# The last 768 tokens' first four chunks as one job of 384-token blocks, in place of a 192-token tile and two 288-token jobs

## Chip, core and metric

The kernel runs on one core of a Trainium2 chip. The metric is the time of one execution on the device in microseconds (us); lower is better. Engines: PE (TensorE) multiplies, DVE (VectorE), ACT (ScalarE) and POOL (GpSimd) work element by element, SP issues the DMA transfers.

## What is computed

Three layers in a row, in float32: causal attention with a bias (4 batches, 8 heads, 576 tokens, 64 wide), then a gated layer with an RMS norm over 2304 tokens (512 to 1536 and back), then a second layer (512 to 2048 and back).

```
scores = q @ k.T / 8 + min(-(cum_i - cum_j), 0), causal; attn = softmax(scores) @ v
x   = attn as 2304 x 512;  xn = x / rms(x) * rms_g
y   = (silu(xn @ w_gate) * (xn @ w_val)) @ w_out
out = gelu_sigmoid(y @ w_in) @ w_out2
```

## The kernel before

Float32 operands are split into a rounded part and a remainder, so that a product is three PE instructions (`mm3`, `mul`). The first layer's 1536 inner columns are 12 chunks of 128; `G0` = 4 of them are done early, as *fill*: while the attention runs, PE takes `fa_tile` products of finished tokens between the heads' own. A fill tile (an entry of `TIN`) has 4 chunks, each with 8 gate and value steps and 4 output steps of three instructions, 144 in all. Tiles 0 to 5 have 256 tokens, the seventh has 192 (tokens 1536 to 1727, the rest of batch 2). A tile's result goes to `y_d` in DRAM through the copy `YO`.

The other tokens are done behind the attention. `TA` = 1728 tokens are covered by tiles; the last 576 are two jobs "R" of `RN` = 288 (`run_r`): gate and value products over 4 row blocks, an activation (`gate`, `gated`, `split_h`), and output products (`Down`), whose result passes through a ring of three buffers `RE` to `r_d`. Chunk 4 of tokens 0 to 767 is a plain job "P" with 384-token blocks, whose gate and value products stand partly among the last fill products. Two short products then clear banks 6 and 7 for what follows.

From there on the jobs of `SJ` run: a job is a layer, a part `p` of 768 tokens and some chunks. Each chunk takes seven block products (`Group`, m1 to m7) in place of eight, on pieces B11 to T4 of the tokens. `piece` makes a piece from `xT` at a part's first use and writes it to `pc_d`; later jobs load it. `load_y` reads a part's early result back into `xT`, to which the outputs are added. Weights come as 64-bit floats and are decoded by ACT, DVE and POOL (`decode`) into 17 slots; a unit is taken up when a slot is free (`tick`, `declare_w`).

The order of each engine's work comes from a planner (`plan`) that places all recorded operations by latest start times; `HD`, `FD` and `WD` are due times for heads, fill tiles and weights. What it chose is fixed in the built program. Profile lines all name L214, the one line through which operations are issued, so the tiles tell them apart: `w` and `s` after the comma are weights, `sc` and `sd` hold the fill's inputs, `sb`, `sf`, `sg`, `sh` the attention's.

```
"TIN": [(t * 256, 256) for t in range(6)] + [(1536, 192)],
RN = (NT - TA) // 2
jobs = [("P", 0, [G0]), ("R", 0, list(range(G0))), ("R", 1, list(range(G0)))] + SJ
```

Of the kernel before, what the change touches and what calls it, by code (L numbers as in the profile page):

```python
# [24 lines left out]
PRM = {  # L25
    "G0": 4, "NWS": 17, "NWO": 12, 
    "QF": set(range(10)), "VF": set(range(10)),
    "TIN": [(t * 256, 256) for t in range(6)] + [(1536, 192)],
    "PPB": 3, "PTB": 8, "XHB": 7, "HHB": 5,
    "VIRT": 260096,  # L30
    "SLOTS": {
# [14 lines left out]
    "TA": 229.33, "PASS": 0, "ISSUE": 0.45, "IDLE": 7, "PEN": {},  # L46
}


# [1 line left out]
def attention_then_swiglu_then_gelu(ctx: ExitStack, tc, qT, kT, vp, s, w1, w2, gT, out):  # L51
# [13 lines left out]
    NW, NWS = 3 * G0, PRM["NWS"]  # L65
    H2 = 384
    NP = NT // (2 * H2)
    RN = (NT - TA) // 2
    NAMES = ["B11", "T1", "T2", "B22", "T3", "B21", "T4"]


# [8 lines left out]
    pq = ctx.enter_context(tc.tile_pool(name="pq", bufs=1, space=PSUM))  # L80
    slots = ctx.enter_context(tc.tile_pool(name="slots", bufs=1, reuse_waits="tile"))
    PB = [pq.tile([P, 512], F32, tag=f"b{i}", name=f"b{i}") for i in range(8)]
    y_d = dram.tile([P, KT, TA], F32, tag="y_d", name="y_d")
    c_d = dram.tile([HB, S], F32, tag="c_d", name="c_d")
    ch_d = dram.tile([HB, 2, S], F32, tag="ch_d", name="ch_d")
    pc_d = {
        (l, p, nm): dram.tile([P, 4 * H2], F32, tag=f"pc{l}{p}{nm}", name=f"pc{l}{p}{nm}")
        for l in "12" for p in range(NP) for nm in NAMES
    }
    r_d = [dram.tile([P, KT, RN], F32, tag=f"r{i}", name=f"r{i}") for i in range(2)]  # L90

    def own(name, shape, dt=F32):
        return const.tile([P] + shape, dt, tag=name, name=name)
# [8 lines left out]
    def few(n):  # L102
# [8 lines left out]
    SHAPE = {  # L111
        "Q": [S], "K": [S], "mask": [S], "SQ": [S], "VS": [5, 2 * D], "PA": [1600], "PT": [512], "VP": [2, 5, 2, D],
        "BT": [320], "XH": [2, TS], "TH": [TS], "FH": [2, TS], "YO": [2, TS], "w": [2, 512], "wb": [512], "ws": [512],
        "MK": [2, 2, H2], "HH": [2, H2], "M5": [H2], "SG": [H2], "V1": [H2], "RE": [RN], **{nm: [2, 2, H2] for nm in NAMES},
    }
    ROUND = ("QA", "QB", "KA", "KB", "VP", "XH", "FH", "w", "HH", *NAMES)

# [49 lines left out]
    def get(name, n=None):  # L167
        if n is None:
            return BUF[name][0]
        return [BUF[f"{name}{i}"][0] for i in range(n)]  # L170
# [9 lines left out]
    PC = {nm: BUF[nm][0] for nm in NAMES}  # L180
    MK, HH, M5, SG = get("MK", 2), get("HH", 8), get("M5", 2), get("SG", 2)
    wb, ws, V1 = (get(x) for x in ("wb", "ws", "V1"))
    RE = get("RE", 3)
    FB = [PB[i] for i in PRM["FB"]]
    BB = [PB[i] for i in PRM["BB"]]

# [193 lines left out]
    def cp(o_, i_, scale=1.0, **kw):  # L380
        op("A", lambda e: e.activation(out=o_, in_=i_, func=AF.Copy, scale=scale), **kw)
# [10 lines left out]
    def dma(o_, i_, eng="S", **kw):  # L392
        op(eng, lambda e: e.dma_start(out=o_, in_=i_), dma=True, **kw)
# [528 lines left out]

    def load_y(p):
        lo, hi = p * 2 * H2, (p + 1) * 2 * H2
        n = min(hi, TA)
        dma(xT[:, :, lo:n], y_d[:, :, lo:n])
        if hi > n:
            for i in range(2):
                t0 = TA + i * RN
                dma(xT[:, :, t0:t0 + RN], r_d[i][:, :, :])  # L930

# [4 lines left out]
    def bank_():  # L936
        return bank_free.pop(0)

    def done(b):
        bank_free.append(b)  # L940

    def tmul(fn):
        op("T", fn, chain=True)
# [13 lines left out]

    hh = {}
    hh_i = [0]
    sg_i = [0]  # L960

    def split_h(key, src, n, psum):
        s = (0, 1, 2, 3, 0, 1)[hh_i[0]] if hh_i[0] < 6 else (hh_i[0] - 2) % 8
# [90 lines left out]
    class Down:  # L1054
# [30 lines left out]
        def finish(self, first, final):  # L1085
            self.part(self.chunks)
            b, p, o = self.b, self.p, self.o
            ps = FB[b]
            if self.layer == "R":
                q = o[1]  # L1090
                t = RE[(q + p * KT) % 3]
                cp(t[:, :RN], ps[:, :RN])
                dma(r_d[p][:, q, :], t[:, :RN])
            elif self.layer == "P":
                t, q = o
                mt = MK[t].rearrange("p a k n -> p (a k) n").bitcast(F32)
                add(mt[:, q, :], ps[:, :H2], mt[:, q, :])
                if q == KT - 1:
                    dma(y_d[:, :, (2 * p + t) * H2:(2 * p + t + 1) * H2], mt)
            elif self.layer == "1":  # L1100
                t, q = o
                y = xT[:, q, (2 * p + t) * H2:(2 * p + t + 1) * H2]
                add(y, ps[:, :H2], y)
            else:
                b0 = p * 2 * H2
                if o < 4:
                    v, src = xT[:, o, b0:b0 + 512], ps[:, :]
                else:
# [16 lines left out]
    for g in range(4):  # L1125
        for p in ((2, 1, 0) if g % 2 == 0 else (0, 1, 2)):
            SJ.append(("2", p, [2 * g, 2 * g + 1]))
    jobs = [("P", 0, [G0]), ("R", 0, list(range(G0))), ("R", 1, list(range(G0)))] + SJ

    def olist(layer, cs):  # L1130
        return [2 * x + y for x in cs for y in (0, 1)] if layer == "2" else cs
# [15 lines left out]

    step[0] = 1
    declare_w()
    for t in range(2):  # L1150
        mt = MK[t].rearrange("p a k n -> p (a k) n").bitcast(F32)
        dma(mt, y_d[:, :, t * H2:(t + 1) * H2])
    first = {"B11": "B11", "B21": "B21", "B12": "T1", "B22": "B22"}
    for nm in ("B11", "B21", "B12", "B22"):
        k, t = BL[nm]
        part2(PC[first[nm]], xv(k, 0, t))
    w = fw["1", G0, "f"]
    for t in range(2):
        bs = [bank_(), bank_()]
        for k, y in enumerate("12"):  # L1160
            for b, r in zip(bs, "12"):
                mul(FB[b], w["A" + r + y], first[f"B{y}{t + 1}"], k == 0, k == 1)
        i = gate(FB[bs[0]], H2)
        done(bs[0])
        gated((G0, t), i, FB[bs[1]], H2)
        done(bs[1])

    RX = [("T2", "T3"), ("T4", "B21")]

    def split_r(i):  # L1170
        t0 = TA + i * RN
        for k in range(2):
            part2(PC[RX[i][k]][:, :, :, :RN], xT[:, 2 * k:2 * k + 2, t0:t0 + RN])

    split_r(0)
    split_r(1)

    def ones():
        for i in range(2):
            tmul(lambda e, i=i: e.matmul(BB[i][:, :], WS[2][:, 0, 0:P], WS[2][:, 0, :], start=True, stop=True))  # L1180

    ones()
    tick()
    for o in [(t, q) for t in range(2) for q in range(KT)]:
        Down("P", 0, o, [G0], H2).finish(True, False)
# [7 lines left out]
        gi[0] += 1  # L1193
        return g

    def run_r(i, ahead):
        downs = [Down("R", i, (0, q), list(range(G0)), RN) for q in range(KT)]
        for c in range(G0):
            bs = []
            for u in range(2):  # L1200
                b = bank_()

                def fn(e, b=b, u=u, c=c):
                    for k in range(KT):
                        x = PC[RX[i][k // 2]]
                        mm3(e, FB[b][:, :RN], WS[3 * c + u], k * P, lambda a: x[:, a, k % 2, :RN], k == 0, k == KT - 1)

                tmul(fn)
                bs.append(b)
            g = gate(FB[bs[0]], RN)  # L1210
            done(bs[0])
            gated((c, 0), g, FB[bs[1]], RN)
            done(bs[1])
            tick()
            if (i, c) == (0, 0):
                for nm in ("B11", "T1", "B22"):
                    piece("1", SJ[0][1], nm)
            if (i, c) == (1, 0):
                for nm in ("T2", "T3"):
                    piece("1", SJ[0][1], nm)  # L1220
            if (i, c) == (1, G0 - 1):
                for nm in ("B21", "T4"):
                    piece("1", SJ[0][1], nm)
        for d in downs[:3]:
            d.part(list(range(G0 - 1)))
        for x, d in enumerate(downs):
            d.finish(True, False)
            for f in ahead.get(x, ()):
                f()
        tick()  # L1230

    run_r(0, {})
    nxt = new_group(SJ[0], 0)
    run_r(1, {0: (nxt.m1,), 1: (nxt.m5,), 2: (nxt.m6,)})
    seen = set()
    for j, job in enumerate(SJ):
        layer, p, cs = job
# [230 lines left out]
```

## Time and profile before

| what | value |
|---|---|
| timed runs, median of 3 | 1048.69 us (1047.87 to 1049.31) |
| the profiled execution: time, span | 1048.84 us, 1047.1 us |
| busy: PE, DVE, ACT, POOL | 1027.7, 704.5, 571.3, 409.9 us |
| instructions | 17466 |

The page's busy share is an average over stages with different limits. The kernel has an attention stage with fill (to about 359 us), a short join, the two "R" jobs (to about 409 us) and the jobs of seven products to the end; they are to be read stage by stage. A matmul's own duration in the trace covers its way through the array and overlaps the next; what one costs in a row of them is the distance between starts.

### The profile page before, as it was taken

To read this page: it belongs to the slowest core of one execution; us is meant where nothing else is said; L and a number is where in the kernel's file an instruction comes from. 1 tells how busy PE (TensorE), PEld (TensorE's weight loads), DVE (VectorE), ACT (ScalarE), POOL (GpSimd) and SP (SyncE) were. 2 spreads that over 40 slices of the span, in tenths; PEclk is the share of its full clock that TensorE was granted. 3 is DMA by queue.
4 is the path that set the end of the run, shared out by engine and by line. 5 is a ranking of instruction groups with operands and counts; after the bars stand their busy time and mean duration, and the time that the engine had idled before them with its cause. 6 is when DMAs were issued, how large, how long until landed. Compare 5 with 4: busy or idle time off the path is not lost.

```text
span 1047.1 us, 17466 instructions
## 1 busy us (share of the span) xinstructions
PE 1027.7 (98%) x6214; PEld 964.5 (92%) x6214; DVE 704.5 (67%) x1590; ACT 571.3 (55%) x1306; POOL 409.9 (39%) x482
## 2 busy tenths in 40 slices
PE   9997999999999999999999999999999999999998
PEld 5886999999999999999999999989999988999987
DVE  6776887778867757888754787876564376373333
ACT  5785886776667435565432444667663244453322
POOL 5656687665546513544310443632230042030000
PEclk9998999999999999999999999999999999999999
DMA  5457665564431645675454287766165237514551
GB/s 152 115 148 180 171 152 159 157 168 114 102 100 39 209 164 203 219 285 181 149 196 179 61 291 271 272 231 251 54 245 200 85 101 271 211 41 145 203 195 61
DMA packets 64639, 176.22 MB, mean 168 GB/s; under 512 B 7284, under 2 KB 26228, under 8 KB 64552
## 3 DMA queue, kind: packets, MB, share of 16 engines
q1 hardware_dynamic: 64440, 175.02, 50.6%
q8 instruction: 49, 0.80, 0.3%
q14 instruction: 38, 0.31, 0.1%
q10 hardware_dynamic: 112, 0.08, 0.0%
HBM read 111.34 MB, written 44.26 MB: 149 GB/s over the span
## 4 chain that ended last, share of the span: by engine, by line
PE 89%; DVE 3%; DMA 3%; POOL 1%; issue 1%; SPq 1%; ACT 0%; DVEq 0%; POOLq 0%; ACTq 0%
PE b L214 89%; POOL s L214 1%; DVE s L214 1%; DMA st<-in_w_dram 1%; DMA s<-in_kT_dram 1%; SPq L214 1%; DMA s<-in_qT_dram 1%; DMA s<-s 0%; DVE xT L214 0%; DVE sg L214 0%; DVE wm L214 0%; DVE sb L214 0%; DVE b L214 0%; DVE sh L214 0%; DVE se L214 0%
## 5 line engine op out<-in xcount | busy, mean ns | idle before, releaser
L214 PE MATMUL b<-s,w 128*128 128x384 f32 (+1 forms) x882 | 167.9, 332 | 0.0
L214 PEld LDWEIGHTS b<-s,w 128*128 128x128 f32 x882 | 152.7, 188 | 0.9 <-DVE s L214 0.3
L214 POOL TENSOR_TENSOR wa<-wa,st 128x512 int32<-128x512 int32 x52 | 71.0, 1365 | 188.3 <-ACT sb L214 60.1
L214 DVE TENSOR_TENSOR xT<-b,xT 128x384 f32<-128x384 f32 (+1 forms) x134 | 79.8, 608 | 83.6 <-PE b L214 82.6
L214 PE MATMUL b<-sc,w 128*128 128x256 f32 (+3 forms) x840 | 132.3, 296 | 1.8 <-DVE se L214 1.2
L214 PEld LDWEIGHTS b<-sc,w 128*128 128x128 f32 x840 | 116.4, 192 | 3.0 <-DVE se L214 1.4
L214 PE MATMUL b<-sd,w 128*128 128x256 f32 (+3 forms) x642 | 113.8, 305 | 0.0
L214 ACT ACTIVATE b<-b 128x384 f32<-128x384 f32 x119 | 55.6, 479 | 98.9 <-DVE b L214 57.0
L214 POOL TENSOR_SCALAR wm<-wm 128x512 f32<-128x512 f32 x68 | 49.1, 722 | 133.8 <-DVE wm L214 123.0
L214 PEld LDWEIGHTS b<-sd,w 128*128 128x128 f32 x642 | 97.6, 189 | 0.3
L214 POOL TENSOR_SCALAR s<-s,small 128x576 f32<-128x576 f32 (+4 forms) x160 | 88.6, 572 | 23.5 <-DVE small L214 18.3
L214 ACT ACTIVATE s<-s,small 128x192 f32<-128x192 f32 (+4 forms) x160 | 88.5, 554 | 16.9 <-DVE small L214 16.6
L214 PE MATMUL b<-s 128*128 128x288 f32 (+5 forms) x398 | 91.9, 356 | 5.6 <-DMA s<-s 2.8
L214 PE MATMUL b<-s,s 128*128 128x384 f32 (+1 forms) x453 | 91.7, 338 | 0.0
L214 PEld LDWEIGHTS b<-s,s 128*128 128x128 f32 x453 | 79.4, 188 | 1.1
L214 DVE CUSTOM_DVE_ANT_0 s<-b,s 128x448 f32<-128x448 f32 (+4 forms) x160 | 64.6, 424 | 20.7 <-PE b L214 19.8
L214 PE MATMUL b<-ident,s 128*128 128x128 f32 x480 | 72.4, 278 | 5.6 <-POOL s L214 5.2
L214 PEld LDWEIGHTS b<-s 128*128 128x128 f32 x398 | 61.4, 195 | 16.6 <-issue 7.6
L214 ACT ACTIVATE se<-b 128x384 f32<-128x384 f32 (+4 forms) x89 | 41.2, 464 | 64.2 <-PE b L214 61.9
L214 PE MATMUL b<-w,sc 128*128 128x512 f32 x270 | 74.2, 390 | 0.0
L214 ACT ACTIVATE sa<-b 128x384 f32<-128x384 f32 (+2 forms) x100 | 44.7, 447 | 52.8 <-PE b L214 27.9
L214 ACT ACTIVATE st<-st 128x512 int32<-128x512 uint32 x68 | 45.6, 674 | 38.3 <-DMA st<-in_w_dram 38.3
(156 smaller groups left out, 2205.0 us busy)
## 6 DMA issues: line engine op xcount, KB each, us to landing
st<-in_w_dram SPq DMA_DIRECT2D x68, 512.0 KB
s<-s SPq DMA_DIRECT2D x132, 144.0 KB
s<-pc21B SPq DMA_DIRECT2D x9, 768.0 KB
s<-pc11B SPq DMA_DIRECT2D x6, 768.0 KB
s<-pc22B SPq DMA_DIRECT2D x6, 768.0 KB
out_dram<-xT SPq DMA_DIRECT2D x18, 256.0 KB
s<-in_vp_dram SPq DMA_DIRECT2D x16, 256.0 KB
s<-in_qT_dram SPq DMA_DIRECT2D x11, 288.0 KB
```

The source lines that it names most:

```text
L214: return lambda *args, **kw: f(*[real(x) for x in args], **{k: real(x) for k, x in kw.items()})
```

## The change

The seventh fill tile and the "R" jobs are taken out. A job "Q" does chunks 0 to 3 for the last part (p = 2, tokens 1536 to 2303) as the plain job does chunk 4: two blocks of 384 tokens, on the pieces B11, B12, B21 and B22. One block's chunk 0 stands ahead of the two clearing products, the rest behind the "P" outputs. Its result goes through the same ring (now 384 columns) to `y_d`, which now holds all tokens, and `load_y` reads it back like the other parts. The pieces B11 and B21 stay as pieces of the first job, which is now of part 2 instead of part 1 (the two change places in `SJ`). The due times have new values; of them the line of `FD` is shown.

```diff
-    "TIN": [(t * 256, 256) for t in range(6)] + [(1536, 192)],
+    "TIN": [(t * 256, 256) for t in range(6)],
...
-    "SJ": [(1, (4, 5)), (1, (6,)), (2, (4, 5, 6)), (0, (5, 6, 7)), (0, (8, 9)), (1, (7, 8, 9)), (2, (7, 8, 9)),
+    "SJ": [(2, (4, 5)), (2, (6,)), (1, (4, 5, 6)), (0, (5, 6, 7)), (0, (8, 9)), (1, (7, 8, 9)), (2, (7, 8, 9)),
...
-    "FD": [(60.43, 220.18), (276.78, 130.22), (354.31, 155.01), (290.61, 374.54), (205.29, 210.44), (220.67, 247.65), (551.21, 276.9)],
+    "FD": [(61.47, 158.14), (298.8, 136.77), (341.97, 163.14), (330.8, 282.67), (226.27, 274.98), (251.66, 331.87)],
...
-    RN = (NT - TA) // 2
-    y_d = dram.tile([P, KT, TA], F32, tag="y_d", name="y_d")
+    y_d = dram.tile([P, KT, NT], F32, tag="y_d", name="y_d")
-    r_d = [dram.tile([P, KT, RN], F32, tag=f"r{i}", name=f"r{i}") for i in range(2)]
...
-            if self.layer == "R":
-                q = o[1]
-                t = RE[(q + p * KT) % 3]
-                cp(t[:, :RN], ps[:, :RN])
-                dma(r_d[p][:, q, :], t[:, :RN])
+            if self.layer == "Q":
+                t, q = o
+                r = RE[re_i[0] % len(RE)]
+                re_i[0] += 1
+                cp(r, ps[:, :H2])
+                dma(y_d[:, q, (2 * p + t) * H2:(2 * p + t + 1) * H2], r)
...
+    def plain(c, t, at):
+        w = fw["1", c, "f"]
+        bs = [bank_(), bank_()]
+        for k, y in enumerate("12"):
+            for b, r in zip(bs, "12"):
+                mul(FB[b], w["A" + r + y], at[f"B{y}{t + 1}"], k == 0, k == 1)
+        i = gate(FB[bs[0]], H2)
+        done(bs[0])
+        gated((c, t), i, FB[bs[1]], H2)
+        done(bs[1])
...
+    blocks(0, at0, ("B11", "B21", "B12", "B22"))
+    plain(G0, 0, at0)
+    blocks(p2, at2, ("B12", "B22"))
+    plain(G0, 1, at0)
+    blocks(p2, at2, ("B11", "B21"))
+    plain(0, 1, at2)
...
-    def run_r(i, ahead):
...
-    run_r(0, {})
+    for c in range(G0):
+        if c:
+            plain(c, 1, at2)
+        if c == G0 - 1:
+            for nm in ("T2", "T3"):
+                piece("1", p2, nm)
+        plain(c, 0, at2)
         tick()
+        if c == 0:
+            kept(p2, "B11")
+            kept(p2, "B21")
+            for nm in ("T1", "B22"):
+                piece("1", p2, nm)
+    piece("1", p2, "T4")
     nxt = new_group(SJ[0], 0)
-    run_r(1, {0: (nxt.m1,), 1: (nxt.m5,), 2: (nxt.m6,)})
+    ahead = {1: nxt.m1, 3: nxt.m5, 5: nxt.m6}
+    for x, o in enumerate([(t, q) for t in (1, 0) for q in range(KT)]):
+        Down("Q", p2, o, list(range(G0)), H2).finish(True, False)
+        if x in ahead:
+            ahead[x]()
```

`blocks` splits the named blocks of a part into rounded part and remainder; `kept` writes a piece that is there already to `pc_d`.

**PE, from the last head's score products on.** Before (`b6` and `b7` with `w0` to `w11` are fill products, `s2` and `s1` score products, `sf`, `sg`, `sh` with `sb` the heads' products with v):

```order
L214 MATMUL b7_73<-sd_0_1035,w2_130 128x256 x3
L214 MATMUL b4_70<-sf_1_1041,sb_0_919 128x320 x2
L214 MATMUL b6_72<-sc_0_937,w0_128 128x192 x3
L214 MATMUL b4_70<-sf_1_1041,sb_0_919 128x256
L214 MATMUL b4_70<-sg_1_1087,sb_0_919 128x256
L214 MATMUL b6_72<-sc_0_937,w0_128 128x192 x3
L214 MATMUL b4_70<-sg_1_1087,sb_0_919 128x128 x2
L214 MATMUL b6_72<-sc_0_937,w0_128 128x192 x6
L214 MATMUL b6_72<-sc_0_937,w1_129 128x192 x6
L214 MATMUL b5_71<-s2_0_738 128x288
L214 MATMUL b5_71<-s1_0_195 128x288
L214 MATMUL b6_72<-sc_0_937,w1_129 128x192 x6
```

In the change:

```order
L212 MATMUL b1_67<-s2_0_755 128x448
L212 MATMUL b1_67<-s1_0_193 128x448
L212 MATMUL b6_72<-sc_0_929,w0_126 128x256 x9
L212 MATMUL b3_69<-ident_120,s8_0_151 128x128 x4
L212 MATMUL b4_70<-sf_1_1047,sb_0_992 128x320 x2
L212 MATMUL b6_72<-sc_0_929,w0_126 128x256 x3
L212 MATMUL b4_70<-sf_1_1047,sb_0_992 128x256
L212 MATMUL b4_70<-sg_1_1089,sb_0_992 128x256
L212 MATMUL b6_72<-sc_0_929,w1_127 128x256 x3
L212 MATMUL b4_70<-sg_1_1089,sb_0_992 128x128 x2
L212 MATMUL b6_72<-sc_0_929,w1_127 128x256 x9
L212 MATMUL b5_71<-s2_0_755 128x288
```

The 192-column products of the seventh tile are gone; 256-column products of the sixth tile, which stood further ahead, are in their place.

**PE, at the join.** Before (`ident` with `small` are the transposes of the last normalization, `b6_72<-w2` and `b7_73<-w2` the clearing products, `sb` the first outputs of "P"):

```order
L214 MATMUL b4_70<-ident_122,small_127 128x64
L214 MATMUL b4_70<-ident_122,small_127 128x128
L214 MATMUL b4_70<-ident_122,small_127 128x64
L214 MATMUL b6_72<-w2_130 128x512
L214 MATMUL b7_73<-w2_130 128x512
L214 MATMUL b4_70<-sb_1_4186,s1_1_3862 128x384 x3
L214 MATMUL b5_71<-sb_1_4186,s1_1_3862 128x384 x3
L214 MATMUL b0_66<-sb_1_4186,s1_1_3862 128x384 x3
```

In the change (`sd_1` and `sg_2` are now blocks B12 and B22 of part 2, `s6_1` and `s7_1` the plain job's blocks):

```order
L212 MATMUL b4_70<-ident_120,small_125 128x64
L212 MATMUL b3_69<-s6_1_3741,s2_1_3901 128x384 x6
L212 MATMUL b7_73<-sd_0_1012,w11_137 128x256 x3
L212 MATMUL b2_68<-s7_1_3813,s1_1_3696 128x384 x6
L212 MATMUL b3_69<-s7_1_3813,s2_1_3901 128x384 x6
L212 MATMUL b4_70<-sd_1_4067,w0_126 128x384 x6
L212 MATMUL b5_71<-sd_1_4067,w1_127 128x384 x6
L212 MATMUL b4_70<-sg_2_4077,w0_126 128x384 x6
L212 MATMUL b5_71<-sg_2_4077,w1_127 128x384 x6
L212 MATMUL b6_72<-w2_128 128x512
L212 MATMUL b7_73<-w2_128 128x512
L212 MATMUL b0_66<-sb_1_4012,s1_1_3696 128x384 x3
```

Before, the outputs follow the transposes with the two clearing products between. Now 18 products of the plain job, 3 of the fill and 24 of "Q" come first, the latter on blocks that DVE and ACT make from the normalized tokens.

**DVE, at the same place.** Before (`xT<-xT,small` is the normalization, `se<-b7` the fill's last copy, `sc_1<-b` the additions of "P"):

```order
L214 SCALAR_TENSOR_TENSOR xT_121<-xT_121,small_127,b4_70 128x320 x4
L214 TENSOR_TENSOR b3_69<-sa_1_4143,b3_69 128x384
L214 TENSOR_SCALAR se_0_1020<-b7_73 128x2x192
L214 SCALAR_TENSOR_TENSOR xT_121<-xT_121,small_127,b4_70 128x256 x4
L214 TENSOR_TENSOR sb_1_4186<-b3_69,sb_1_4186 128x384
L214 TENSOR_TENSOR sd_1_4263<-xT_121,sd_1_4263 128x2x288
L214 TENSOR_TENSOR sc_1_4106<-b4_70,sc_1_4106 128x384
L214 TENSOR_TENSOR sc_1_4106<-b5_71,sc_1_4106 128x384
```

In the change:

```order
L212 TENSOR_TENSOR b1_67<-sa_1_3980,b1_67 128x384
L212 TENSOR_SCALAR wm_124<-st1_122 128x512
L212 SCALAR_TENSOR_TENSOR xT_119<-xT_119,small_125,b4_70 128x320 x4
L212 TENSOR_TENSOR sb_1_4012<-b1_67,sb_1_4012 128x384
L212 TENSOR_TENSOR s3_1_3559<-xT_119,s3_1_3559 128x768
L212 SCALAR_TENSOR_TENSOR xT_119<-xT_119,small_125,b4_70 128x256 x4
L212 TENSOR_SCALAR se_0_987<-b7_73 128x512
L212 TENSOR_TENSOR sd_1_4067<-xT_119,sd_1_4067 128x768
L212 TENSOR_TENSOR sg_2_4077<-xT_119,sg_2_4077 128x768
L212 TENSOR_TENSOR b3_69<-sa_1_3980,b3_69 128x384
L212 TENSOR_TENSOR sb_1_4012<-b3_69,sb_1_4012 128x384
```

Two subtractions of 768 columns (`sd_1`, `sg_2`) stand ahead of the second gated product (`b3_69`), and one (`s3_1`, block B11) between the two halves of the normalization.

## Rows read from the trace of the kernel before

**Rows 1.** The page, busy time of the engines over the span.
```profile
PE 1027.7 (98%) x6214; PEld 964.5 (92%) x6214; DVE 704.5 (67%) x1590; ACT 571.3 (55%) x1306; POOL 409.9 (39%) x482
```

**Rows 2.** Stages: from:to and length, busy us (count) of five engines, clock, DMA share, GB/s.
```profile
120.00:180.00 60.00, 58.13 (x473) 56.28 (x472) 51.76 (x154) 46.28 (x125) 48.05 (x62) 1.00 0.62 164
...
232.30:316.00 83.70, 82.00 (x674) 80.57 (x672) 64.21 (x196) 54.20 (x149) 44.66 (x66) 1.00 0.39 100
...
359.20:361.15 1.95, 0.79 (x4) 0.40 (x3) 1.95 (x6) 1.74 (x4) 1.95 (x2) 1.00 0.91 234
...
361.10:367.00 5.90, 5.85 (x25) 5.88 (x26) 5.50 (x9) 1.31 (x2) 5.17 (x4) 0.71 0.51 203
...
410.00:443.00 33.00, 32.31 (x182) 31.05 (x181) 27.64 (x51) 19.27 (x37) 16.01 (x11) 1.00 0.64 223
...
443.00:1043.50 600.50, 600.46 (x3182) 564.28 (x3180) 366.17 (x644) 279.00 (x563) 154.74 (x137) 1.00 0.50 183
```

**Rows 3.** The chain that ended last: start us, length us, what (and pieces).
```profile
409.50 10.13 DMA st<-in_w_dram
...
442.00 601.48 PE b L214 x3186
```

**Rows 4.** PE in order of time (start us, us, instruction, count), then one stage.
```profile
318.18 1.53 PE L214 MATMUL b<-sc,w 128*128 128x192 f32 x12
319.55 0.45 PE L214 MATMUL b<-s 128*128 128x288 f32 x2
...
350.33 0.81 PE L214 MATMUL b<-sd,w 128*128 128x192 f32 x6
350.98 1.23 PE L214 MATMUL b<-s,s 128*128 128x384 f32 x6
...
366.98 0.95 PE L214 MATMUL b<-sg,w 128*128 128x288 f32 x6
367.76 0.95 PE L214 MATMUL b<-sd,w 128*128 128x288 f32 x6
368.56 0.95 PE L214 MATMUL b<-sg,w 128*128 128x288 f32 x6
...
480.00:580.00 100.00, 100.00 (x579) 100.00 (x578) 60.00 (x117) 41.37 (x86) 19.96 (x22) 1.00 0.45 165
```

**Rows 5.** Groups of PE and DVE, 232.3 to 316 us: busy us, mean ns | idle before.
```profile
L214 PE MATMUL b<-sc,w 128*128 128x256 f32 x264 | 37.7, 286 | 0.4 <-POOL sc L214 0.4
...
L214 PE MATMUL b<-sd,w 128*128 128x256 f32 x96 | 16.0, 289 | 0.0
...
L214 DVE SCALAR_TENSOR_TENSOR se<-se,b 128x256 f32<-128x256 f32 x12 | 5.0, 417 | 4.8 <-ACT se L214 4.8
...
L214 DVE TENSOR_TENSOR se<-se,b 128x256 f32<-128x256 f32 x11 | 4.6, 418 | 0.2
...
L214 DVE TENSOR_TENSOR sc<-xT,sc 128x256 fp32r<-128x256 f32 x4 | 3.5, 914 | 0.2 <-ACT sc L214 0.2
...
L214 DVE TENSOR_TENSOR sd<-se,sd 128x256 fp32r<-128x256 f32 x3 | 2.3, 783 | 0.2 <-ACT sd L214 0.2
...
L214 DVE TENSOR_SCALAR se<-b 128x512 f32<-128x512 f32 x2 | 1.4, 692 | 1.6 <-PE b L214 1.6
```

**Rows 6.** The join, 341 to 363 us: DVE and PE in order of time, PE's wait.
```profile
341.26 0.96 DVE L214 TENSOR_TENSOR s<-xT,s 128x768 fp32r<-128x768 f32 x1
...
354.98 1.92 DVE L214 SCALAR_TENSOR_TENSOR xT<-xT,small,b 128x320 f32<-128x320 f32 x4
...
358.55 0.72 PE L214 MATMUL b<-ident,small 64*128 64x64 f32 x3
...
359.35 1.65 DVE L214 SCALAR_TENSOR_TENSOR xT<-xT,small,b 128x256 f32<-128x256 f32 x4
...
361.38 1.80 DVE L214 TENSOR_TENSOR sd<-xT,sd 128x576 fp32r<-128x576 f32 x1
...
PE b L214 <- DVE xT L214: 1.2, 1, 1.2
```

More of the change, by code (lines that the diff above doesn't have):

```diff
@@ L40 @@
     "RQ": "AVG", "RV": "VG", "NORM": "G",
[1 row of a table removed]
[1 row of a table added]
            (2, (10, 11)), (1, (10, 11)), (0, (10, 11))],
[3 rows of a table removed]
-    "TA": 229.33, "PASS": 0, "ISSUE": 0.45, "IDLE": 7, "PEN": {},
[3 rows of a table added]
+    "TA": 227.54, "REB": 3, "PASS": 0, "ISSUE": 0.45, "IDLE": 7, "PEN": {},
 }
@@ L113, in attention_then_swiglu_then_gelu @@
         "BT": [320], "XH": [2, TS], "TH": [TS], "FH": [2, TS], "YO": [2, TS], "w": [2, 512], "wb": [512], "ws": [512],
-        "MK": [2, 2, H2], "HH": [2, H2], "M5": [H2], "SG": [H2], "V1": [H2], "RE": [RN], **{nm: [2, 2, H2] for nm in NAMES},
+        "MK": [2, 2, H2], "HH": [2, H2], "M5": [H2], "SG": [H2], "V1": [H2], "RE": [H2], **{nm: [2, 2, H2] for nm in NAMES},
     }
@@ L182, in attention_then_swiglu_then_gelu @@
     wb, ws, V1 = (get(x) for x in ("wb", "ws", "V1"))
-    RE = get("RE", 3)
+    RE = get("RE", PRM["REB"])
     FB = [PB[i] for i in PRM["FB"]]
@@ L924, in load_y @@
         lo, hi = p * 2 * H2, (p + 1) * 2 * H2
[L925 to L930, printed above, removed]
+        dma(xT[:, :, lo:hi], y_d[:, :, lo:hi])
     bank_free = list(range(6))
@@ L959, in attention_then_swiglu_then_gelu @@
     hh_i = [0]
-    sg_i = [0]
+    sg_i, re_i = [0], [0]
     def split_h(key, src, n, psum):
@@ L1127, in attention_then_swiglu_then_gelu @@
             SJ.append(("2", p, [2 * g, 2 * g + 1]))
-    jobs = [("P", 0, [G0]), ("R", 0, list(range(G0))), ("R", 1, list(range(G0)))] + SJ
+    jobs = [("P", 0, [G0]), ("Q", NP - 1, list(range(G0)))] + SJ
     def olist(layer, cs):
@@ L1149, in attention_then_swiglu_then_gelu, with blocks @@
     declare_w()
+    for c in range(G0):
+        fw["1", c, "f"] = {"A11": (3 * c, 0), "A12": (3 * c, 256), "A21": (3 * c + 1, 0), "A22": (3 * c + 1, 256)}
+    def plain(c, t, at):
[8 more added lines that the diff above has]
+        done(bs[1])
+    def blocks(p, at, names):
+        for nm in names:
+            k, t = BL[nm]
+            part2(PC[at[nm]], xv(k, p, t))
     for t in range(2):
@@ L1152, in attention_then_swiglu_then_gelu @@
         dma(mt, y_d[:, :, t * H2:(t + 1) * H2])
[L1153 to L1182, printed above, removed]
+    at0 = {"B11": "B11", "B21": "B21", "B12": "T1", "B22": "B22"}
+    at2 = {"B11": "B11", "B21": "B21", "B12": "T3", "B22": "T2"}
+    p2 = NP - 1
+    blocks(0, at0, ("B11", "B21", "B12", "B22"))
[4 more added lines that the diff above has]
+    plain(0, 1, at2)
+    for i in range(2):
+        tmul(lambda e, i=i: e.matmul(BB[i][:, :], WS[2][:, 0, 0:P], WS[2][:, 0, :], start=True, stop=True))
     tick()
@@ L1194, in new_group, with kept @@
         return g
-    def run_r(i, ahead):
[L1197 to L1229, printed above, removed]
-        tick()
-    run_r(0, {})
-    nxt = new_group(SJ[0], 0)
-    run_r(1, {0: (nxt.m1,), 1: (nxt.m5,), 2: (nxt.m6,)})
+    def kept(p, nm):
+        made.add(("1", p, nm))
+        dma(pc_d["1", p, nm][:, :], flat(PC[nm]))
+    for c in range(G0):
+        if c:
[4 more added lines that the diff above has]
+        plain(c, 0, at2)
+        tick()
+        if c == 0:
[4 more added lines that the diff above has]
+    piece("1", p2, "T4")
+    nxt = new_group(SJ[0], 0)
+    ahead = {1: nxt.m1, 3: nxt.m5, 5: nxt.m6}
[3 more added lines that the diff above has]
+            ahead[x]()
+    tick()
     seen = set()
```

4 rows, old and new, of the table PRM are left out of this document.

## The prediction

> **What bounds the kernel now.** I read the page's busy times first: PE is busy for 1027.7 of 1047.1 us [rows 1], so a change to PE's own work moves the end almost one for one, and the question is where PE still waits. The table by stage answers it [rows 2]. From 443 us on, 600.50 us hold 600.46 us of PE: nothing waits there, and the chain runs through PE alone for 601.48 us [rows 3]. The losses lie in three places: in the attention (58.13 of 60 us around 150 us, 82.00 of 83.70 us in the heads 25 to 31), at the join behind the last head (359.2 to 367 us), and in the first jobs of seven products (32.31 of 33 us). The change touches all three, and the pace of some products. The profiled execution took 1048.84 us, 0.15 us over the median of the three timed runs; my sums start from 1048.84. About 0.2% (2.1 us) is what a measurement of this kernel can tell from no change.
>
> **Part 1, the products themselves.** The seventh tile goes: 4 chunks x 12 x 3 = 144 products of 192 columns, in the attention stage. The two remainder jobs go: 288 products of 288 columns. In their place stand 192 products of 384 columns for gate and value and 96 for the output. The columns are the same before and after, 110,592; only the cuts differ. What a product costs is read from starts [rows 4]: twelve of 192 columns take 319.55 - 318.18 = 1.37 us, six take 350.98 - 350.33 = 0.65 us, that is 0.114 and 0.108 us each, and I use 0.111. Six of 288 columns take 368.56 - 367.76 = 0.80 us, and twelve from 366.98 take 1.58 us: 0.1317 us each. 579 products of 384 columns fill 100.00 us: 0.1727 us each. So 144 x 0.111 = 16.0 us leave the attention, 288 x 0.1317 = 37.9 us leave the stretch behind it, and 288 x 0.1727 = 49.7 us come there: **-4.2 us** on PE (bounds -3.8 and -4.7, by 0.108 and 0.114).
>
> A rule speaks against this. The Trainium skill ("TensorE: Matmul & The Clock Gate", Back-to-back issue gap) gives a lone product N / 2.4 + 2.5 ns: 82.5, 122.5 and 162.5 ns for the three widths, by which this part would be worth 144 x 2.5 ns, 0.4 us. The trace disagrees with the first of them (108 and 114 ns). The same section says of a stream that weight load and product set the spacing together, and the page's section on LDWEIGHTS puts a load at columns / 1.2, an estimate of 107 ns for 128; with that the trace agrees.
>
> **Part 2, the attention with one tile less.** The order of PE tells where the fill products go. From the first score of the 12th head to that of the 25th it has 456 fill products before and 456 now. From there to the first score of the last head it has 360 (264 + 96, [rows 5]) before and 222 now. Behind that, 144 of 192 and 48 of 256 columns give way to 186 of 256, about as long. So the 16.0 us are taken out of one stretch, 232.3 to 316 us, which would go from 83.7 to 67.7 us if PE stayed as dense. VectorE must keep up: it is busy for 64.21 us there [rows 2], of which the fill's operations are 5.0 + 4.6 + 3.5 + 2.3 + 1.4 = 16.8 us [rows 5]; 138 of 360 products take 6.4 us of them along, which leaves 57.8 of 67.7 us, 85%, where 77% stands today. The nearest row of such a load is 120 to 180 us: VectorE 51.76 of 60, 86%, and PE still busy for 97%. PE's idle time by that row would be 2.1 us of 67.7, against 1.70 us now: +0.4 us. The other end: VectorE's share stays at 77%, the stretch takes 57.8 / 0.767 = 75.4 us, +7.7 us. I take **+2.0**, nearer the row with the same load, since small waits below PE's busy row come on top of it.
>
> **Part 3, the join.** Before, the last transposes start at 358.55 us and end by 359.2; two short products that clear banks 6 and 7 follow, and then PE waits 1.2 us for VectorE's normalization, which reads bank 4, the bank of the first output product [rows 6]. Of the 1.95 us from 359.20 PE is busy for 0.79 [rows 2], and two products of 512 columns at the pace above would want 0.45: 1.5 us lost. Then the granted clock is 0.71 over 5.90 us from 361.10 [rows 2], partly at the lower of its two levels (1.2 GHz), and the 24 products up to 366.98 [rows 4] take 5.83 us where 24 x 0.1727 = 4.1 would do: 1.7 us more, 3.2 in all. Now 24 products of columns 1920 to 2303 stand ahead of those two, and they need bank 4 and VectorE's remainder sd, which comes behind the same normalization. VectorE's queue from the first half of it: about 1.0 of other work, 1.92 (four scalings), 0.55 (384 columns, between the 0.42 of 256 and the 0.69 of 512), 0.96 (768 columns), 1.65 (four scalings), 0.69 (the fill's copy) and 0.96, together 7.7 us, or 8.6 if the last goes at 1.80 beside GpSimd, as the one at 361.38 did [rows 5, 6]. PE has in the meantime 21 fill products of 256 columns (2.6 us, at a pace between the 0.111 of 192 and the 0.132 of 288 columns), 3 transposes (0.6), 18 products of 384 columns (3.1) and 3 more of the fill (0.4): 6.7 us. sd is late by 1.0 to 1.9 us; I take 1.2, and half of today's clock loss, 0.9: 2.1 for 3.2, **-1.1** (ends -3.2 and +1.5: no wait at all, or a wait of 3 us with today's clock loss in full). Behind that wait stand the two clearing products and the output products of chunk 4; nothing overtakes it on PE.
>
> **Part 4, the first jobs.** In 410 to 443 us PE runs 182 products, 31.4 us at full pace, in 33: 1.6 us lost. The chain there holds 10.13 us of a weight transfer [rows 3], queued with a read-back of 1.5 MB. Now about 50 us rather than 41 lie between the join and the first job, and the slots of chunks 0 to 3 come free earlier in them, so units are decoded with more lead. But the read-back is now of the very rows that this job has just written, and VectorE's queue still waits for a unit behind it. **-0.5** (ends -1.6 and +2).
>
> **At nothing:** the eight copies into the ring and eight writes (384 instead of 288 columns, ScalarE 19.27 of 33 us busy in the first jobs [rows 2]; and a ring buffer is wanted again only after three output groups, 3 x 12 x 0.1727 = 6.2 us; if a write took longer, the copy and with it a bank would wait). The kept pieces B11 and B21 save two roundings; their writes and the one read-back in place of three hardly change SP's queue, 465 transfers for 469. The swapped jobs have the same products; their cover is the dense stretch from 443 us.
>
> **Sum:** -4.2 + 2.0 - 1.1 - 0.5 = -3.8: 1045.0 us.
>
> **The rivals.** (a) *VectorE cannot be packed denser* (slower). The last heads stay at its 77%, +7.7, and the join is as late as today: -4.2 + 7.7 - 0.5 = +3.0, 1051.8 us. It is slower by over 0.2% once the heads lose more than about 6.8 us, a share below 78%. For it: what PE waited for there is an element-wise result (0.4 us for GpSimd before a fill product [rows 5]). Against: 86% has been reached at 120 to 180 us. 18%. (b) *More comes back*: the heads lose nothing, join and first jobs stop waiting: -4.2 - 3.2 - 1.6 = -9.0, 1039.8 us. For it: cover and lead both grow. Against: sd's arithmetic. 13%. (c) *Only columns count*: a 192-column product is slow because others stand between, not by itself, and cutting differently gives nothing: 0 + 2.0 - 1.1 - 0.5, 1049.2 us. The Trainium skill's rule for the lone product (TensorE: Matmul & The Clock Gate, Back-to-back issue gap) would make nearly this of it. Against: twelve in a row with nothing between take 0.114. 5%. (d) *The read-back ends late*: the last copy (0.5), a write, the 1.5 MB (1.57 million bytes) at the 223 GB/s of 410 to 443 us [rows 2] (7.0), and a unit's 10.13 ahead or in between make 18 us and more, and PE has 108 products, 18.7 us, until it wants the first bank back. If it is 4 us late: 1049.0 us. 8%.
>
> **How the numbers follow.** The forecast's own case has 56% and runs from 1042 to 1047.5 us. Faster by over 0.2%: 50 of its 56 and (b), 63%. Within 0.2%: the rest of it, (c), most of (d) and the mild end of (a), 19%. Slower: 18%, from (a) and the far end of (d). The range that leaves out half of (b) and about half of (a) is 1040.0 to 1051.5.
>
> **What would show it.** Right: no 192- or 288-column product beside the scores, 288 more of 384 at 0.173; first score of the last head near 302 us with VectorE at about 85% in the 68 us before; PE waiting 1 to 2 us for sd; PE dense from the first job's end to the last product, as before. Wrong: the last heads' stretch at 73 us or more, a clock drop of several windows at the join, or PE waiting for xT in the first job.

## The result, and the profile after

The change takes 1037.74 us (median of 4 runs, 1036.68 to 1040.27) against 1048.28 us before (median of 4 runs, timed with it): the ratio is 0.990, with an interval of 0.988 to 0.993. That is 10.5 us gained where 3.8 were forecast, and it lies below the range (1040.0 to 1051.5). The profiled execution of the change is its slowest run, 1040.27 us (span 1038.5); against the profiled execution before, 1048.84 us, 8.6 us of the gain are to be seen in it. The page's first line, which answers to [rows 1], and the stages, which answer to [rows 2]:

```profile
PE 1022.5 (98%) x6070; PEld 960.2 (92%) x6070; DVE 697.6 (67%) x1573; ACT 569.3 (55%) x1299; POOL 407.1 (39%) x472
```

```profile
231.40:297.30 65.90, 64.85 (x528) 63.35 (x528) 55.78 (x178) 50.96 (x139) 40.49 (x58) 1.00 0.48 121
297.30:341.62 44.32, 43.88 (x339) 42.81 (x339) 35.35 (x85) 28.84 (x60) 22.69 (x27) 1.00 0.31 104
341.62:346.27 4.65, 4.65 (x27) 4.55 (x27) 4.09 (x7) 2.74 (x5) 3.27 (x2) 1.00 0.42 156
346.27:350.45 4.18, 4.18 (x25) 4.17 (x24) 3.85 (x9) 0.49 (x1) 4.10 (x3) 1.00 0.90 366
350.45:400.00 49.55, 49.55 (x287) 49.55 (x287) 28.84 (x53) 23.19 (x44) 16.93 (x16) 1.00 0.51 171
400.00:435.00 35.00, 34.02 (x196) 33.44 (x195) 27.15 (x46) 17.65 (x34) 13.04 (x9) 1.00 0.52 202
435.00:1034.00 599.00, 599.00 (x3175) 563.06 (x3173) 364.29 (x641) 277.17 (x561) 148.92 (x130) 1.00 0.50 182
```

The stretches are cut where PE reaches the same point of the program in both: the score product of 448 columns of the 25th head (232.3 us before, 231.4 now; this is what the prediction called its first score), that of the last head (316.0 and 297.3), the first output product of chunk 4 (361.15 and 346.27), their end (366.98 and 350.45), PE's last product (1043.1 and 1034.2).

| stretch | before | after | difference | forecast |
|---|---|---|---|---|
| up to the 25th head | 232.3 | 231.4 | -0.9 | 0 |
| heads 25 to 31 | 83.7 | 65.9 | -17.8 | -16.0 + 2.0 = -14.0 |
| last head to the first output of chunk 4 (24 products more) | 45.15 | 48.97 | +3.8 | +3.0 for these two |
| the 24 outputs of chunk 4 | 5.83 | 4.18 | -1.65 | (24 x 0.1727 = 4.1, join -1.1) |
| from there to PE's last product | 676.1 | 683.75 | +7.65 | 264 x 0.1727 - 37.9 - 0.5 = +7.2 |
| sum | 1043.1 | 1034.2 | -8.9 | -3.8 |

The row to look at is the first of the stages: VectorE has come to 55.78 of 65.90 us, the 85% that the prediction worked out, and PE stands idle for 1.05 us in it where it stood idle for 1.70 before [rows 2]. Twelve products of 256 columns in a row, with the start of what follows them, give their pace in this stretch as (282.19 - 280.75) / 12 = 0.120 us:

```profile
280.75 1.59 PE L212 MATMUL b<-sc,w 128*128 128x256 f32 x12
282.19 0.60 PE L212 MATMUL b<-ident,s 128*128 128x128 f32 x4
```

So the 138 products that left it are worth 16.6 us. The other 1.2 us are less sharp. By PE's busy time 0.65 us of waiting went with the products. And both heads start with six narrower score products, about a microsecond ahead of the mark; counted from the first of these (231.6 to 314.8 us before, 230.3 to 296.5 now) the stretch gave 17.1 us in place of 17.8. What PE waited for in it (in total, times, longest), before and now:

```profile
PE b L214 <- POOL s L214: 1.3, 1, 1.3
PE b L214 <- POOL sc L214: 0.4, 1, 0.4
```

```profile
PE b L212 <- DVE xT L212: 0.7, 1, 0.7
PE b L212 <- issue: 0.3, 1, 0.3
```

The join, PE in order of time:

```profile
334.66 2.77 PE L212 MATMUL b<-sd,w 128*128 128x256 f32 x21
...
338.01 1.31 PE L212 MATMUL b<-s,s 128*128 128x384 f32 x6
...
340.76 1.03 PE L212 MATMUL b<-s,s 128*128 128x384 f32 x5
341.62 2.27 PE L212 MATMUL b<-sd,w 128*128 128x384 f32 x12
343.73 2.24 PE L212 MATMUL b<-sg,w 128*128 128x384 f32 x12
345.81 0.63 PE L212 MATMUL b<-w 128*128 128x512 f32 x2
346.27 4.34 PE L212 MATMUL b<-sb,s 128*128 128x384 f32 x24
```

VectorE makes the second half of the normalization (xT) from 338.11 us on; the remainder sd is started at 340.64 us and done 0.96 us later:

```profile
333.96 0.55 DVE L212 TENSOR_TENSOR b<-sa,b 128x384 f32<-128x384 f32 x1
...
338.11 1.66 DVE L212 SCALAR_TENSOR_TENSOR xT<-xT,small,b 128x256 f32<-128x256 f32 x4
...
340.64 0.96 DVE L212 TENSOR_TENSOR sd<-xT,sd 128x768 fp32r<-128x768 f32 x1 [0.24 <-ACT sd L212]
```

PE takes it up at 341.62, with no gap behind the five products before. What fills the time of the second normalization is 18 products of the plain job and 3 of the fill, which run behind the last transposes (338.01 to 341.62 us); before, those of the plain job stood ahead of the transposes. The 24 products of the job "Q" come behind them. The two clearing products cost 0.46 us, and the granted clock is 1.00 all through, where it was 0.71 [rows 2].

Behind the join the chain of waits shows one stop before PE runs alone:

```profile
426.81 0.74 ACT sg L212
427.62 2.13 POOL sg L212
429.80 604.82 PE b L212 x3203
```

The weight transfer of 10.13 us [rows 3] is no longer in it; a GpSimd split of the first job took its place, and PE is idle there for 0.98 of 35 us (before for 0.69 of 33 [rows 2]).

### The profile page after: what moved, and what is told of

Same layout as the page of the kernel before. It is cut to its first block, busy times and chain, and to the rows that moved or that the text cites. A ratio compares the mean times of both kernels' runs of the same rounds, so it can differ in the third digit from the quotient of the medians.

```text
span 1038.5 us, 17144 instructions
## 1 busy us (share of the span) xinstructions
PE 1022.5 (98%) x6070; PEld 960.2 (92%) x6070; DVE 697.6 (67%) x1573; ACT 569.3 (55%) x1299; POOL 407.1 (39%) x472
## 4 chain that ended last, share of the span: by engine, by line
PE 95%; DMA 1%; DVE 1%; SPq 1%; issue 0%; ACT 0%; POOL 0%; DVEq 0%; ACTq 0%
PE b L212 95%; SPq L212 1%; DMA s<-s 1%; DMA s<-in_kT_dram 0%; DVE s L212 0%; DMA s<-in_qT_dram 0%; DVE xT L212 0%; POOL sg L212 0%; DVE sd L212 0%; ACT s L212 0%; ACT sg L212 0%; DVE sh L212 0%; DVE wa L212 0%; ACT sa L212 0%; DVE small L212 0%
## 5 line engine op out<-in xcount | busy, mean ns | idle before, releaser
L212 PE MATMUL b<-s,w 128*128 128x384 f32 x930 | 177.6, 334 | 0.0
L212 PEld LDWEIGHTS b<-s,w 128*128 128x128 f32 x930 | 163.0, 188 | 0.6
L212 PE MATMUL b<-sc,w 128*128 128x256 f32 (+1 forms) x744 | 122.5, 301 | 0.0
L212 PEld LDWEIGHTS b<-sc,w 128*128 128x128 f32 x744 | 106.5, 192 | 0.9 <-issue 0.2
L212 PE MATMUL b<-sd,w 128*128 128x384 f32 (+1 forms) x594 | 107.3, 312 | 0.1
L212 PEld LDWEIGHTS b<-sd,w 128*128 128x128 f32 x594 | 92.7, 189 | 0.8 <-DVE sd L212 0.3
L212 ACT ACTIVATE s<-s,small 128x576 f32<-128x576 f32 (+4 forms) x160 | 88.3, 554 | 7.7 <-DVE small L212 7.2
L212 DVE CUSTOM_DVE_ANT_0 s<-b,s 128x192 f32<-128x192 f32 (+4 forms) x160 | 64.3, 424 | 19.5 <-PE b L212 18.9
L212 ACT ACTIVATE sa<-b 128x384 f32<-128x384 f32 (+1 forms) x100 | 45.0, 452 | 47.6 <-DVE b L212 26.9
L212 ACT ACTIVATE se<-b 128x384 f32<-128x384 f32 (+2 forms) x82 | 38.3, 469 | 58.8 <-PE b L212 52.2
```

The costliest lines, as they stand in the source:

```text
L212: return lambda *args, **kw: f(*[real(x) for x in args], **{k: real(x) for k, x in kw.items()})
```

## The experiments

Ratios are against the kernel before, timed beside each run. Where a text says "the change" it means 1037.8 us: the change run once more (e5, below) gave 1037.83. "Due times" are the tables `HD`, `WD`, `FD` and `TA`, from which the planner derives the order. Waiting of PE in the attention is summed from the distances between PE's starts up to 360 us, less the pace of each width: 28.7 us before, 26.3 and 22.5 in the two profiles of the change. What the lower clock level costs is counted in it. By PE's busy time alone, the idle time up to 360 us is 14.0 us before and 11.2 and 10.6 in the change. Fill products by the heads they stand in are counted in the same way, from all of PE's starts.

**e1, the change with the due times of before.**

```diff
-    "FD": [(61.47, 158.14), (298.8, 136.77), (341.97, 163.14), (330.8, 282.67), (226.27, 274.98), (251.66, 331.87)],
+    "FD": [(60.43, 220.18), (276.78, 130.22), (354.31, 155.01), (290.61, 374.54), (205.29, 210.44), (220.67, 247.65)],
...
```

> The changed kernel with the due times of the kernel before (HD, WD, TA, and the first six of FD); the work is the same, only the order differs. Theory A (PE's own work bounds the last heads, so a removed fill product comes back in full wherever the planner puts the rest): within 2.5 us of the change, 1036 to 1040 us. Theory B (the work alone gives the forecast's -4, the other 6 us come from the new due times): 1043 to 1046 us.

1054.31 us, ratio 1.007 (1.005 to 1.008): both theories missed. The same work in the old order is slower than the kernel before. PE waits 38.7 us in the attention. The groups of fill products in the heads 12 to 16, here:

```profile
L212 PE MATMUL b<-sc,w 128*128 128x256 f32 x192 | 30.6, 299 | 0.0
L212 PE MATMUL b<-sd,w 128*128 128x256 f32 x66 | 10.9, 291 | 0.5 <-ACT se L212 0.5
```

and in the change:

```profile
L212 PE MATMUL b<-sc,w 128*128 128x256 f32 x120 | 19.6, 308 | 0.0
L212 PE MATMUL b<-sd,w 128*128 128x256 f32 x18 | 3.0, 291 | 0.0
```

258 fill products are used up where the change takes 138, and the heads behind them lack cover. There the chain runs through a head's preparation (start, length, what), and the granted clock falls to its lower level for 6.8 us at 269.6:

```profile
257.93 2.68 DMA s<-in_kT_dram
260.69 0.66 POOL s L212
261.43 0.78 POOL s L212
...
266.22 2.65 DMA s<-s
```

```profile
255.00:285.00 30.00, 27.73 (x195) 26.05 (x194) 21.93 (x78) 19.72 (x57) 20.58 (x29) 0.89 0.66 166
```

**e6, the kernel before with the due times of the change** (the diff of e1 the other way round, the seventh tile's times kept).

> The kernel before with the due times of the change (HD, WD, TA, six entries of FD; the seventh tile keeps its own). Theory B (the new due times are better in themselves): faster than before, 1041 to 1046 us. Theory C (due times fit one set of work; in place, the fills cover the heads' waits, and out of place PE waits): slower than before, 1053 to 1062 us.

1053.31 us, ratio 1.005 (1.003 to 1.006). The new times are not better ones; each set fits one set of work. Exchanging them costs 16.5 us one way and 5.0 the other. No run has due times searched anew for the kernel before, so whether its own were the best for it, and how much of the gain in the attention is a better fit, stays open.

**e2, the join put back: the block of chunk 0 that stood ahead of the clearing products stands behind the outputs of chunk 4.**

```diff
     blocks(p2, at2, ("B11", "B21"))
-    plain(0, 1, at2)
...
     for c in range(G0):
-        if c:
-            plain(c, 1, at2)
+        plain(c, 1, at2)
```

> The changed kernel with the 24 products of the first block moved from ahead of the two clearing products to behind the output products of chunk 4. Theory A: the wait for bank 4 behind the last normalization comes back (1.2 to 1.9 us) and with it one stretch at the lower clock (1.7 us): 1040 to 1042 us, 2.5 to 4 us over the change. Rival (the cover is not needed, the planner finds other products for that place): less than 1 us over the change.

1048.57 us, ratio 1.001 (1.000 to 1.002), well over both expectations. The edit moved the planner's placing of the heads as well, and PE waits 32.8 us in the attention. So it was made again with due times searched anew.

**e8, as e2, with due times fitted to it.**

> The changed kernel with the 24 products moved behind the output products of chunk 4, with due times searched anew for it. Theory C: the heads go back to the change's level, the join costs its wait and one stretch at the lower clock (2.5 to 4 us): 1040 to 1043 us. If the join cover is worth nothing by itself: 1036 to 1039 us. If the earlier loss was not in the due times: 1046 us or more.

1044.29 us, ratio 0.996 (0.995 to 0.998), 6.5 us over the change and 1.3 over the expectation. In the profiles it is 5.5 us: 3.8 in the attention up to the last transposes (342.2 us; the change reaches that point, in the profile of e5, at 334.9, with 18 products of 384 columns and 3 of the fill fewer ahead of it, 3.5 us), 1.7 behind. Without the block of "Q" there, the planner put the 18 products of the plain job ahead of the transposes again. The stage of the clearing products and the outputs:

```profile
342.20:344.20 2.00, 0.92 (x5) 0.41 (x4) 1.98 (x6) 1.31 (x3) 1.83 (x1) 1.00 0.95 366
344.20:348.50 4.30, 4.30 (x25) 4.30 (x26) 4.30 (x9) 2.13 (x4) 3.40 (x2) 1.00 0.75 303
```

1.1 us of waiting for xT are back, as before; the lower clock is not.

**e3, only the cut: the kernel before with six tiles and two "R" jobs of 384 tokens.**

```diff
-    "TIN": [(t * 256, 256) for t in range(6)] + [(1536, 192)],
+    "TIN": [(t * 256, 256) for t in range(6)],
...
-        dma(xT[:, :, lo:n], y_d[:, :, lo:n])
+        if n > lo:
+            dma(xT[:, :, lo:n], y_d[:, :, lo:n])
```

> The kernel before with the seventh tile taken out and its two remainder jobs on 384 tokens each; old due times, old order of the jobs, no block ahead of the clearing products, no kept pieces. Theory A: widths and missing tile give their part (-4 in pace and about -2 more in the heads), the join stays as before: 1041 to 1043 us. Theory B (due times): 1044 to 1047 us.

1060.04 us, ratio 1.012 (1.011 to 1.013). Both theories missed. It has the old due times, and shows what e1 shows: 258 fill products in the heads 12 to 16, 41.9 us of waiting in the attention. At the join PE waits for xT in two stops, 3.8 us in all, and the lower clock level follows for 3.4 us from 356.1.

**e7, as e3, with due times fitted to it.**

> The kernel of the run with two 384-token jobs, with due times searched anew for it (HD, FD, WD). Theory C: the waits in the heads go back to about what the kernel before has, so pace and missing tile count (-4) and the join stays (0): 1042 to 1046 us. Rival D (with 144 fill products less the heads cannot be covered, whatever the due times): still 1050 us or more.

1051.76 us, ratio 1.003 (1.002 to 1.005), past theory C's end by 5.8 us and where theory D had it. Waiting in the attention falls by 10 us, to 31.9, but the first jobs lose 3.7 of 40 us, where the change loses 0.98 of 35:

```profile
405.00:445.00 40.00, 36.31 (x199) 35.66 (x198) 32.35 (x52) 19.89 (x38) 20.26 (x15) 0.96 0.60 216
```

The longest wait of PE there is for VectorE's split sg (435.98 us, 2.58 in the chain), and a lower clock follows it (3.4 us from 439.8). So the cut alone does not give the change's time. Which of the change's parts protects its first jobs (the kept pieces, the part that comes first, the weights' order) was not separated. Nor need the search for due times have found the best ones for e7 and e8, so what the single parts are worth is bounded by these runs and not measured.

**e5, the change again.**

> The changed kernel once more, unaltered, for a second profile and more times beside the next three: 1036 to 1040 us. If the first profile (the slowest of its runs) stands for all, its stages repeat within 1 us; if a typical run is shorter, the profile names the stage.

1037.83 us, ratio 0.990 (0.989 to 0.992). Its profile is 2.5 us shorter than the first one of the change, and 2.3 of these lie before the 17th head (144.6 us against 146.9), where the order is the same: executions of one order differ by that much. The granted clock goes with it: at its lower level for 10.2 us between 85 and 102 us in the first profile, for 6.8 in this one; and of the change's eight timed runs the shortest (1036.68 us) has a mean granted clock of 0.997, the longest (1040.27) 0.995. Heads 25 to 31 take 65.20 us, PE busy for 64.95.

```profile
229.10:294.30 65.20, 64.95 (x528) 63.30 (x527) 55.54 (x178) 50.24 (x138) 40.52 (x58) 1.00 0.49 124
```

**e9 and e10, VectorE loaded: one or two more operations behind each of the fill's 24 activations, everything else in the order of the change.**

```diff
-                tt(th, th, v, ALU.mult, eng="V")
+                def scaled(e):
+                    e.tensor_tensor(out=th, in0=th, in1=v, op=ALU.mult)
+                    if isinstance(e, Real):
+                        for _ in range(1):
+                            e.tensor_tensor(out=th, in0=th, in1=th, op=ALU.max)
+
+                op("V", scaled)
```

> The change, with one more VectorE operation behind each of the 24 activations of the fill (a maximum of th with itself, 128x256, which leaves its value; about 0.41 us like the product before it). The order of all other instructions is the change's. 10 us of VectorE are added in the attention, 8 x 0.41 = 3.3 us in the 65.9 us between the heads 25 and 31 (85% busy becomes about 90%). Theory E (VectorE has room at 85%, because the fill products stand between a head's own steps and cover its delays): 1037.5 to 1040.5 us. Theory F (at 85% VectorE already sets the pace of the heads, so that my +2.0 was only too large): most of the 10 us come back, 1044 us or more.

> As the run before, with two more operations behind each activation: 20 us more of VectorE in the attention, 6.6 in the stretch of the last heads (85% becomes about 95%). Theory E: 1039 to 1046 us, with the loss beginning in the last heads. Theory F: 1052 us or more, a microsecond for nearly every one added.

1040.66 us (ratio 0.993, 0.992 to 0.994) and 1050.08 us (1.002, 1.001 to 1.003). The 24 added operations of e9 took 15.5 us, 0.65 each in the mean rather than 0.41 (last section). The heads 25 to 31, of e9 and of e10:

```profile
228.70:295.30 66.60, 64.99 (x528) 63.35 (x527) 60.27 (x186) 50.54 (x139) 40.31 (x58) 1.00 0.48 122
```

```profile
239.40:308.10 68.70, 65.92 (x527) 63.49 (x527) 64.38 (x194) 50.35 (x138) 40.39 (x56) 1.00 0.47 118
```

In this stretch theory E holds: at VectorE's 90% PE loses 1.61 us and at 94% 2.78, against 1.05 in the first profile of the change and 0.25 in e5, and 8.6 us more of VectorE make the stretch 2.8 us longer than in that first profile (3.5 than in e5). Over the whole attention the room is smaller. The first operation (15.5 us) costs 2.8 us against e5, the second (15.4 more) costs 9.4. In the profiles most of that lies ahead of the 25th head, which comes 10.3 us later than in e5, and the granted clock falls to its lower level twice more there (at 70.3 and 169.3 us, 3.4 us each). The profile of e10 is its slowest run, 3.2 us over its median, so these 10.3 us are more than a typical run has. So e9 ends 0.2 us past theory E's range and e10 between the two theories: the first load is mostly hidden, the second mostly not.

**e4, the change with one fill tile less: the sixth tile's products are left out, and its rows of `y_d` are written from the normalized attention.**

```diff
+        if j in (5,):
+            dma(y_d[:, :, t0:t0 + n], xT[:, :, t0:t0 + n])
+            return
```

> The changed kernel with the first-layer products of the sixth fill tile (tokens 1280 to 1535) left out; their rows of y_d are written from the normalized attention instead. 144 products of 256 columns at 0.120 us, 17.3 us of PE, are missing. Theory A (PE bounds the last heads even now): all of it comes back, 1019 to 1022 us. Rival (VectorE, 85% busy in the last heads, takes over): at most 12 us come back, 1026 us or more.

1036.04 us, ratio 0.989 (0.988 to 0.990): of 17.3 us of PE work only 1.7 come back. The heads 25 to 28 keep 24 fill products (123 in the change), and PE has nothing to do while a head's rows are moved: 2.9 of its 4.5 us of idle time here are waits for a DMA, 1.5 for VectorE.

```profile
240.00:260.00 20.00, 15.53 (x78) 12.80 (x78) 15.88 (x65) 12.99 (x38) 13.45 (x23) 0.74 0.81 207
```

```profile
245.94 2.29 DMA s<-in_vp_dram
...
252.08 2.65 DMA s<-s
```

With the waits the granted clock falls to its lower level, for 10.2 us between 246.1 and 259.8; that is a part of what did not come back. So the time lies where the expectation's rival had it, but PE waits here more for the DMA than for VectorE, the cause that it named.

**e11, as e4, with due times fitted to it.**

> The change with the sixth tile's products left out as in the earlier run with one tile less (its rows of y_d are written from the normalized attention, so the outputs of 256 tokens differ), and with due times searched anew for what is left. 17.3 us of PE work are gone. Theory C (due times fit one set of work; refitted, the heads can give more fill away): 5 to 11 us come back, 1027 to 1033 us. Theory G (the due times alone held it all back): 1019 to 1024 us. Theory H (the heads need the fill that the change has as cover, whatever the due times): 1033 to 1037 us.

1032.47 us, ratio 0.986 (0.984 to 0.987), 5.3 us below the change. PE waits 33.7 us in the attention, 11 more than in e5, now at 120 to 160 and 200 to 220 us, each with the lower clock level for 3.4 us:

```profile
120.00:160.00 40.00, 35.41 (x268) 33.59 (x266) 33.43 (x99) 30.65 (x84) 29.83 (x42) 0.96 0.62 161
200.00:220.00 20.00, 17.18 (x128) 16.64 (x127) 14.53 (x48) 13.71 (x38) 9.75 (x15) 0.91 0.60 153
```

The time lies in theory C's range, 0.5 us from theory H's. Due times account for a part of what the missing tile held back (3.6 us between e4 and e11), and 12 of the 17.3 us stay lost. The search need not have found the best times, so these 12 are an upper bound. No kernel that computes the whole result was faster than the change.

## Why the prediction was wrong

**The products (-4.2): right.** Behind the outputs of chunk 4 the change costs 7.65 us, and 264 x 0.1727 - 37.9 = 7.7 was the forecast for the products alone. The paces of 0.1727 us and of 0.1317 us, read from the kernel before [rows 4], carry over. By rival (c), only columns count, the attention would have given up no more than came back behind it, 49.7 - 37.9 = 11.8 us; 17.8 went.

**The attention (+2.0): the step that failed.** The prediction priced the heads' loss by VectorE's share, between the row at 86% and a share kept at 77%. VectorE did come to 85%, yet PE's idle time in the stretch fell (1.70 to 1.05 us) where the sum had a loss of 2.0, and the last head's mark came at 297.3 us, not near 302. Term and measurement are 3.8 us apart: 2.0 of loss that did not come, up to 1.2 of waits that went, and 0.6 of products that now stand behind the last head's scores. A further 0.9 lie ahead of the stretch; in e5 the 25th head comes another 2.3 us earlier in the same order, so the 0.9 are within what two executions differ by. The runs show what the share does not tell. At the same order of work, VectorE at 90% costs 0.7 to 1.4 us of these 66 and at 94% 2.8 to 3.5 (e9, e10), so rival (a) was wrong by mechanism there, not by luck. The runs fit another account: what counts is whether a fill product is at hand when a head waits for its preparation or for VectorE. No run moved single fill products to show this wait by wait. With 864 fill products in place of 1008 that can go either way: in the order that the old due times give, PE waits 10 us more than before (e1), in the order of the change it waits 2 to 6 us less. And the room is not endless: one tile fewer costs two thirds of what its products are worth (e11). The order of PE was there to be read before; it was read for where fill products left, and not for which of the waits of before had lost or gained their cover.

**The join (-1.1): right in kind, too small.** The prediction let sd come 1.0 to 1.9 us late; it came on time, at the end of the five products before it, and PE went from the transposes to the outputs without a stop. VectorE's queue took the 7.7 us that were reckoned (333.9 to 341.6 us), and PE's products took 7.0 in place of 6.7; but the reckoning let both begin together, and PE began its 21 fill products only at 334.66, about 0.8 us after VectorE. The whole 3.2 us went: the 1.5 us of waiting, and the clock loss. About 1.2 us came back behind the last head's first score, half of it in fill products (186 x 0.120 in place of 144 x 0.111 + 48 x 0.120 us), so the two stretches together gave +2.15 for a forecast of +3.0. Of the fitted kernel with the old order at the join (e8) 1.7 us lie behind the last transposes. That the wait brings the lower clock with it is not shown: e8, e2 and e7 have the wait, and no lower level follows there.

**The first jobs (-0.5): not seen in the time.** The chain lost its weight transfer, as argued. By the prediction's reckoning at full pace PE's loss went from 1.6 of 33 us to 1.15 of 35 (196 products at 0.1727); by its idle time it rose from 0.69 to 0.98. Behind the outputs of chunk 4 as a whole, the +7.65 of the table are what the products alone cost, where +7.2 was forecast with this term. The late read-back, rival (d), did not come: PE does not wait for xT between 350 and 445 us.

**Rival (b) was nearest** (1039.8 us: heads that lose nothing, join and first jobs without waits), with 13%. Its price in the attention was bounded at zero, though; a gain there, from fewer waits, was excluded without a reason, and the range left out half of this rival. The profiled execution of the change, the slowest of its runs at 1040.27 us, would have been in the range; the median is 2.5 us below that run, and seven of the eight timed runs of the change lie below 1040.0.

## What to carry to other kernels

Work that fills another stage's gaps has two prices: its own time, and the waits that it covers. When some of it is taken away, list the waits of that stage and look in the new order for what stands in each of them; the busy share of an engine, here 85 and 90%, did not tell that. And bound such a term below zero too: the order around it is made anew, and can lose less than before.

## What the runs showed of the hardware

- An operation of VectorE with both inputs in SBUF took 0.62 us in the mean (th with itself, 128x256) where the same shape with one input in PSUM took 0.41. The two groups in e9, heads 25 to 31:

```profile
L212 DVE TENSOR_TENSOR se<-se 128x256 f32<-128x256 f32 x8 | 4.9, 618 | 0.3
...
L212 DVE TENSOR_TENSOR se<-se,b 128x256 f32<-128x256 f32 x8 | 3.3, 413 | 0.0
```

  It is not the operation that is slow: 14 of the 24 in e9 took 0.42 to 0.44 us and the others 0.54 to 1.50. In e10 a pair takes 0.89 us where GpSimd stands idle beside it. In another pair the first took 1.46 us, until 0.28 us behind the end of a GpSimd product (243.27 us), and the second, with GpSimd idle, 0.42:

```profile
242.09 1.46 DVE L212 TENSOR_TENSOR se<-se 128x256 f32<-128x256 f32 x1
...
243.59 0.42 DVE L212 TENSOR_TENSOR se<-se 128x256 f32<-128x256 f32 x1
...
276.64 0.89 DVE L212 TENSOR_TENSOR se<-se 128x256 f32<-128x256 f32 x2
```

```profile
241.84 1.43 POOL L212 TENSOR_TENSOR s<-s 128x576 fp32r<-128x576 f32 x1
...
276.40 0.20 POOL L212 TENSOR_SCALAR small<-small 128x5 f32<-128x5 f32 x1 [0.18 <-ACT s L212]
277.62 0.41 POOL L212 TENSOR_SCALAR sd<-se 128x256 fp32r<-128x256 f32 x1 [1.02 <-DVE se L212]
```

  The Trainium skill says so ("SBUF — State Buffer", SBUF: two separate sides): VectorE with two SBUF inputs and a GpSimd operation that reads SBUF take one pair of ports in turn, whole instructions long. These rows agree.
- The same wait at the join (1.1 to 1.2 us for xT) was followed by the lower clock level in two profiles of the kernel before's order (the profile before, and e6 at 367.4 us, 3.4 us each) and by none in e2, e7 and e8. What tells them apart stays open.
